# RetNet attention and SwiGLU on one Trainium2 core: the first chunk of the gate's weights loaded later, and products without a use in TensorE's first stops

## The chip, the cores and the metric

The kernel runs on one core of a Trainium2 chip. The metric is the device time of one execution in microseconds (us). Before the change the median of 7 executions is 1141.08 us, from 1139.92 to 1148.08.

A core has a matrix engine (TensorE; in the profile PE, and PEld for its loading of stationary operands), VectorE (DVE), ScalarE (ACT), GpSimd (POOL) and SyncE (SP). Each takes its instructions in an order fixed in the program. In this kernel SP issues nearly all transfers between the chip's memory and the core's own; ScalarE issues a few.

## The reference

Two blocks follow each other. The first is retention without a softmax, with a decay that depends on the head; the second normalizes and applies a gated feed-forward.

```python
# q, k, v: (8, 8, 576, 64) float32: batch, heads, sequence, head size
scores = (1 / sqrt(64)) * q @ k.T
gamma  = 1 - 2 ** (-5 - arange(8))                 # one per head
Dmat   = where(i >= j, gamma ** (i - j), 0)
attn   = (scores * Dmat) @ v
x      = attn.transpose(0, 2, 1, 3).reshape(4608, 512)

xn  = x / sqrt(mean(x * x) + 1e-6) * rms_g
g   = xn @ w_gate                                  # 512 x 1536
out = (g * sigmoid(g) * (xn @ w_val)) @ w_out      # 1536 x 512
```

q, k and v are float32. The three weights arrive in 64-bit floating point (a float32 array times a 64-bit scalar), and the kernel turns them into float32 itself; this is what it calls rounding.

## The kernel before

**Attention jobs.** A job is one batch entry and one pair of heads: 32 jobs of 576 positions. A job runs in chunks of 64 positions with a state carried from chunk to chunk. Its steps, with the line of each: `turn` transposes q and k on TensorE (L228, L234, L242) and ScalarE copies them out of the accumulator banks (L239, L248); `scale_v` multiplies v by the decay on ScalarE (L264); `scores` (L284) and `states` (L304) are products of TensorE; `weigh` masks the scores on VectorE (L316); `sums` carries the states from chunk to chunk on VectorE (L331, L333); `values` (L355) and `carried` (L377) are TensorE's products for the output, and VectorE scales that into x (L397). The scores and states of a job share one set of three accumulator banks, of which there is one, so the next job's `scores` wait for `sums`. `values` of a job is issued in the slot of the next one, and `carried` behind that job's states.

**The feed-forward** works on units of 384 tokens, twelve in all. The first two are multiplied in the plain way (`up_plain`, L614, products of 128x384); the ten others with seven block products in place of eight (`up`, L557, and `across`, L688).

**The start** (function `start`) does the first 8 jobs, which fill units 0 and 1, then the plain products of these two units. In these 8 jobs SP loads everything in an order written out by hand: for each job q, two halves of k, the tails of q and k where they are due, two halves of v, the tail of v (`load_first`, L158, L165, L198). A tail is the last 64 positions; the first tails load is for heads 0 and 1, the second, in job 1, for the six others of the batch entry. Between the jobs come tables and some weights.

**The weights.** They are loaded in 18 chunks of 1024 KB (`load_chunk`, L795): for each third g of the feed-forward's width gate first half, gate second half, value first half, value second half (chunks 0 to 11), then w_out (12 to 17). A 64-bit chunk needs a place of its own while it is rounded, and there are four. `load_chunks(n)` loads on to chunk n as far as places are free.

**Rounding** is a generator, `rounding`, that issues a chunk in steps: the exponent on VectorE (L811), which also enters three operations for ScalarE in a list (Relu, L827); three mantissa steps on VectorE (L838, L843, L848), the third of which needs the three Relus and frees the place, so that a later chunk's load is issued behind it; and the join (L856). `weights(n)` takes n steps, `weights_to(n)` goes on until n chunks are done, `act(n)` issues n of the listed Relus, and all these are called at fixed places of the program. So the place of each step among an engine's other work is fixed.

At the end of job j the kernel calls `turn(j + 1)`, adds the square of x, scales a later v, calls `act(1)`, takes the steps of `weights` for this job, and calls `act(1)` again. In `up_plain` two steps are taken behind each product; the first two products (of the four in a group) use one chunk, the last two the next one. The first group's third product therefore needs chunk 1 joined.

At the very start six products of a matrix of ones with itself run on TensorE into a bank that nobody reads (L920).

Of the kernel before, what the change touches and what calls it, by code (L numbers as in the profile page):

```python
# [14 lines left out]
P = 128  # L15
# [7 lines left out]
def _decay_tables(H, D):  # L23

    pairs = _gamma(H).reshape(H // 2, 2).T
    rows = np.repeat(pairs, D, axis=0)
    pos = np.arange(L)
    p = np.concatenate([pos, pos])  # L30
    gq = rows[:, :, None] ** (pos + L) / np.sqrt(D)
    t = pairs.T[None] ** -p[:, None, None], rows**L, gq, np.roll(gq, D, axis=0)
    return [np.ascontiguousarray(x).astype(np.float32) for x in t]


def _causal_table():

    return np.ascontiguousarray(np.tile(np.triu(np.ones((L, L), np.float32)), (2, 1)))
# [3 lines left out]
def kernel(  # L42
# [11 lines left out]
    nc = tc.nc  # L54
# [33 lines left out]
    def bank(name):  # L88
        return banks.tile([P, 512], F32, tag="b", name=name)
# [9 lines left out]
    ones = const.tile([P, P], F32, name="ones")  # L99
# [117 lines left out]
            out=t, in_=v[b, 2 * hp : 2 * hp + 2, NFULL * P :].rearrange("e p d -> p e d")  # L217
        )

    def turn(j):  # L220

        d = st[j]
        last = bank(f"turn_{j}_t")
        for nm in "qk":
            ps = bank(f"turn_{j}_{nm}")
            for c in range(NFULL):
                if nm == "k":
                    nc.tensor.transpose(  # L228
                        out=ps[:, c * P : c * P + P],
                        in_=d["k"][:, c].rearrange("p e d -> p (e d)"), identity=ident,  # L230
                    )
                    continue
                for e in range(2):
                    nc.tensor.matmul(  # L234
                        ps[side(e), c::NFULL], lhsT=d["q"][:, e, c], rhs=ident,
                        start=True, stop=True,
                    )
            t = d[nm + "T"] = att.tile([P, S], F32, tag=nm + "T", name=f"{nm}T_{j}")
            nc.scalar.copy(out=t[:, : NFULL * P], in_=ps)  # L239
        for i, nm in enumerate("qk"):  # L240
            o = slice(i * TAIL, i * TAIL + TAIL)
            nc.tensor.transpose(  # L242
                out=last[:, o], in_=d[nm + "t"].rearrange("p e d -> p (e d)"),
                identity=ident[:TAIL, :TAIL],
            )
        for i, nm in enumerate("qk"):
            o = slice(i * TAIL, i * TAIL + TAIL)
            nc.scalar.copy(out=d[nm + "T"][:, NFULL * P :], in_=last[:, o])  # L248
# [10 lines left out]
    def scale_v(j):  # L259
        d = st[j]  # L260
        hp = jobs[j][1]
        for e in range(2):
            for t in (d["v"][:, :, e], d["vt"][:, e]):
                nc.scalar.activation(  # L264
                    out=t, in_=t, func=AF.Copy, scale=gv[: t.shape[0], hp, e : e + 1]
                )
# [4 lines left out]
    def side(i):  # L271
        return slice(i * L, i * L + L)
# [489 lines left out]
    for g in range(NG):  # L762
        for m, src in enumerate((moe_w_gate, moe_w_val)):
            for half in range(2):
                n = (half * NH + 2 * g) * P
# [13 lines left out]
    def spare(i):  # L779

        return i % 4 if i < n_up else LATER[i - n_up]

    def load_chunk(i, queue):
        dst, src, rws, cols = chunks[i]
        if src.dtype != F32:
            n = dst.shape[1]
            cols = slice(2 * (cols.start or 0), 2 * cols.stop if cols.stop else None)
            src = src.bitcast(U32)
            at = spare(i)
            dst = free[:, : 4 * DM] if at == 3 else (  # L790
                w_out[:, 4 * at : 4 * at + 4].rearrange("p c f -> p (c f)")
            )
            dst = words_of[i] = dst.bitcast(U32).rearrange("p (c f) -> p c f", c=n)
            waits_at[at] = i
        queue.dma_start(out=dst, in_=src[rws, cols].rearrange("(c p) f -> p c f", p=P))  # L795

    def load_chunks(n, queue=nc.scalar):

        nonlocal n_loads
        while n_loads < min(n, len(chunks)) and waits_at.get(spare(n_loads)) is None:  # L800
            load_chunk(n_loads, queue)
            n_loads += 1
# [90 lines left out]
    def weights(n):  # L893

        for _ in range(n):
            next(steps, None)

    def weights_to(n):

        while n_chunks < min(n, len(chunks)):  # L900
            next(steps)
# [3 lines left out]
    def start():  # L905

        h_of[0] = ffn.tile([P, NF, U], F32, tag="h", name="h_0")
        tables = list(zip((causal, gv, gc, gq, gx), (_causal_table(), *_decay_tables(H, D))))

        def table(i, queue):  # L910
            t, values_ = tables[i]
            src = nc.inline_tensor(values_, name=t.tensor.name + "_table")
            queue.dma_start(out=t, in_=src.ap())

        make_identity(nc, ident)
        nc.scalar.activation(out=tick, in_=mhalf[:1], func=AF.Silu)
        nc.vector.memset(ones, 1.0)
        warm = bank("warm")
        for _ in range(6):
            nc.tensor.matmul(warm[:, :P], lhsT=ones, rhs=ones, start=True, stop=True)  # L920
        first_places.update(find_places())
        load_chunks(1)
        for i in (1, 0, 2):
            table(i, nc.scalar)
        weights(3)
        for j in range(2 * NHP):
            load_first(j, {0: range(2), 1: range(2, H), NHP: range(H)}.get(j))
            if j == 1:
                table(3, nc.sync)
            load_chunks((1, 1, 1, 1, 2, 2, 2, 3)[j], nc.sync)  # L930
        table(4, nc.sync)
        nc.sync.dma_start(out=rms_g, in_=moe_rms_g.rearrange("(c p) -> p c", p=P))
        load_chunks(4, nc.sync)
        turn(0)
        scale_v(0)
        act(3)
        squares = []
        for j in range(2 * NHP):
            slot(j)
            if j + 1 < 2 * NHP:  # L940
                turn(j + 1)
            if squares:
                gather(*squares.pop())
            for i in ((1,), (2,), (3,), (4, 5), (6,), (7,), (), ())[j]:
                scale_v(i)
            if j:
                u, c = divmod(j - 1, NHP)
                squares.append((u, c, square(u, c)))
            act(1)
            if j == 5:  # L950
                norm_1(0)
            elif j == 6:
                norm_2(0)
            weights((2, 0, 0, 1, 1, 1, 1, 0)[j])
            if j == 4:
                gather(*squares.pop())
            elif j == 5:
                diagonals(0)
            act(1)
        gather(*squares.pop())  # L960
        load_qk(2 * NHP)
        load_kv(2 * NHP)
        made = combine_out()
        for m, g in [(m, g) for g in range(NG) for m in range(2)]:
            for u in range(2):
                weights_to(4 * g + 2 * m + 1)
                for i, _ in enumerate(up_plain(u, m, g)):
                    if not (u or m or g):
                        if i == 0:
                            values(2 * NHP - 1)  # L970
                            carried(2 * NHP - 1)
                            gather(1, NHP - 1, square(1, NHP - 1))
                        elif i == 1:
                            norm_1(1)
                        elif i == 2:
                            diagonals(1)
                        elif i == 3:
                            norm_2(1)
                    weights(2)
                    act(1)  # L980
                    if u and m and g == NG - 1:
                        weights_to(len(chunks))
                        next(made, None)
                    if i == 1:
                        weights_to(4 * g + 2 * m + 2)
        for _ in made:
            pass
        for blk, t in first_blocks.items():
            keep(blk, t)
        rest = across(1)  # L990
        next(rest)
        following(2 * NHP - 1)
        for i, _ in enumerate(rest):
            if i == 1:
                norm_0(2)
                differences(0)
            elif i == 2:
                norm_1(2)
                diagonals(2)
            elif i == 4:  # L1000
                norm_2(2)
        rest = across(0)
        next(rest)
        combine(1)
        slot(8, rest=False)
        following(8)
        for _ in rest:
            pass
        combine(0)
        slot(9)  # L1010
        following(9)
# [18 lines left out]
    with tc.manual_schedule():  # L1030
# [4 lines left out]
        for u in range(2, NU):  # L1035
# [11 lines left out]
            for i, _ in enumerate(rest):  # L1047
                if i == 0 and turns:
                    prepare_next(turns.pop())
                if i == 2:  # L1050
                    behind(u, 6)
                    at, n = SLOTS[u % 3]
# [33 lines left out]
```

## Time and profile before

| what | value |
|---|---|
| median of 7 executions | 1141.08 us |
| lowest, highest | 1139.92, 1148.08 us |
| the profiled execution | 1141.87 us |
| its span, first to last instruction | 1140.1 us |
| mean granted clock of TensorE | 0.997 |
| ScalarE's stop before its first copy of q (L239) | 6.70 us |
| VectorE's stop before the exponent of chunk 0 (L811) | 5.69 us |
| ScalarE's stop for the v of job 5 | 1.57 and 0.45 us |
| first product of the feed-forward (L614) starts at | 59.41 us |

The page gives the busy time of each engine, the span in 40 slices, and the costliest groups. The chain of waits follows the work that ended last back to its start, each piece with its start, its length and what it was; "issue" is time for which the profile shows no cause. In the timeline each row has start, length, engine, line, operation, tiles (out<-in), shape and count, and in brackets the idle time ahead of it with what ended it. Times are in us from the first instruction.

### The profile page before, as it was taken

What the parts mean: (1) busy time and instruction counts of PE and PEld (TensorE: products, weight loads), DVE (VectorE), ACT (ScalarE), POOL (GpSimd) and SP (SyncE); (2) the same over time, 40 slices, a digit from 0 to 9 for tenths busy, and PEclk for the clock granted to TensorE, in tenths of its full rate; (3) what the DMA queues carried; (4) which work ended last, traced back from release to release, by engine and by line L of the source; (5) the groups of instructions that cost most, each with busy time, mean ns of one, the idle gap of its engine ahead of it and who ended that gap; (6) DMA issues with size and microseconds to landing.
All of it is one profiled execution on the core that took longest, in us unless ns stands there. A gap on an engine that the chain in (4) does not pass through costs nothing.

```text
span 1140.1 us, 24713 instructions
## 1 busy us (share of the span) xinstructions
PE 1119.1 (98%) x10470; PEld 1046.2 (92%) x10470; DVE 726.6 (64%) x1431; ACT 258.9 (23%) x508; POOL 39.7 (3%) x64
## 2 busy tenths in 40 slices
PE   7899999999999999999999999999999999999998
PEld 6755557999999999999999999999999999999998
DVE  5788868655685685375767676466676666446352
ACT  5546642002212211211221121121121220120210
POOL 0000000470000000000000000000000000000000
PEclk9999999999999999999999999999999999999999
DMA  9764336335464475053444555216436503303304
GB/s 204 209 183 152 110 113 205 62 66 131 102 134 88 125 151 152 1 117 92 103 126 62 127 135 122 113 32 119 115 81 142 139 26 97 126 1 100 124 1 111
DMA packets 292942, 125.40 MB, mean 110 GB/s; under 512 B 270432, under 2 KB 275808, under 8 KB 292832
## 3 DMA queue, kind: packets, MB, share of 16 engines
q1 hardware_dynamic: 282688, 107.66, 38.4%
q10 hardware_dynamic: 10144, 16.16, 4.5%
q8 instruction: 82, 1.34, 0.5%
q14 instruction: 28, 0.23, 0.1%
HBM read 108.83 MB, written 14.94 MB: 109 GB/s over the span
## 4 chain that ended last, share of the span: by engine, by line
PE 93%; DMA 2%; DVE 2%; ACT 1%; issue 1%; SPq 0%; DVEq 0%; POOL 0%; POOLq 0%; ACTq 0%
PE x L557 14%; PE w L557 14%; PE z L557 14%; PE xo L688 8%; PE wo L688 8%; PE zo L688 8%; PE up L614 8%; PE y L557 7%; PE yo L688 4%; PE av L355 2%; PE av L377 2%; PE s L284 1%; PE s L304 1%; DMA w_gate<-in_moe_w_out_dram 1%; PE ms L475 1%
## 5 line engine op out<-in xcount | busy, mean ns | idle before, releaser
L581 ACT COPY m<-x 128x384 f32<-128x384 f32 x60 | 28.8, 479 | 338.8 <-PE x L557 338.8
L688 PE MATMUL xo<-h,w_out 128*128 128x192 f32 x528 | 90.3, 328 | 0.0
L557 PE MATMUL w<-sums,w_val 128*128 128x192 f32 x480 | 88.6, 328 | 0.3
L557 PE MATMUL x<-x,w_val 128*128 128x192 f32 x480 | 88.7, 328 | 0.0
L557 PE MATMUL z<-x,w_gate 128*128 128x192 f32 x480 | 87.9, 326 | 0.7 <-DVE u L564 0.7
L557 PE MATMUL x<-x,w_gate 128*128 128x192 f32 x480 | 88.5, 328 | 0.0
L557 PE MATMUL z<-x,w_val 128*128 128x192 f32 x480 | 87.8, 326 | 0.0
L557 PE MATMUL w<-sums,w_gate 128*128 128x192 f32 x480 | 87.8, 326 | 0.0
L688 PEld LDWEIGHTS xo<-h,w_out 128*128 128x128 f32 x528 | 85.9, 190 | 0.6
L688 PE MATMUL wo<-h,w_out 128*128 128x192 f32 x504 | 85.3, 326 | 0.0
L564 DVE TENSOR_TENSOR u<-m,y 128x384 f32<-128x384 f32 x60 | 33.2, 553 | 79.1 <-PE y L557 79.1
L688 PEld LDWEIGHTS wo<-h,w_out 128*128 128x128 f32 x504 | 82.5, 190 | 0.0
L557 PEld LDWEIGHTS w<-sums,w_val 128*128 128x128 f32 x480 | 79.2, 190 | 2.7 <-DVE c L564 2.7
L557 PEld LDWEIGHTS z<-x,w_gate 128*128 128x128 f32 x480 | 79.6, 190 | 1.0 <-issue 1.0
L557 PEld LDWEIGHTS x<-x,w_val 128*128 128x128 f32 x480 | 79.1, 190 | 0.6
L557 PEld LDWEIGHTS x<-x,w_gate 128*128 128x128 f32 x480 | 79.3, 190 | 0.5
L557 PEld LDWEIGHTS z<-x,w_val 128*128 128x128 f32 x480 | 79.6, 190 | 0.0
L557 PEld LDWEIGHTS w<-sums,w_gate 128*128 128x128 f32 x480 | 79.5, 190 | 0.0
L564 DVE TENSOR_TENSOR h<-u,w 128x384 f32<-128x384 f32 x60 | 33.1, 551 | 69.5 <-PE w L557 69.4
L576 ACT ACTIVATE h<-h 128x384 f32<-128x384 f32 x90 | 47.0, 523 | 89.5 <-DVE h L564 89.5
L614 PE MATMUL up<-x,w_gate 128*128 128x384 f32 x192 | 63.3, 488 | 0.9 <-DVE x L526 0.7
L614 PE MATMUL up<-x,w_val 128*128 128x384 f32 x192 | 62.7, 487 | 0.1
(187 smaller groups left out, 1769.8 us busy)
## 6 DMA issues: line engine op xcount, KB each, us to landing
w_out<-w_blocks SPq DMA_DIRECT2D x70, 768.0 KB, 5.0
out_dram<-o SPq DMA_DIRECT2D x368, 24.0 KB, 1.6
qraw<-in_q_dram SPq DMA_DIRECT2D x96, 72.0 KB, 2.8
kraw<-in_k_dram SPq DMA_DIRECT2D x96, 72.0 KB, 2.8
k<-in_k_dram SPq DMA_DIRECT2D x48, 128.0 KB, 3.0
v<-in_v_dram SPq DMA_DIRECT2D x48, 128.0 KB, 3.1
w_out<-in_moe_w_gate_dram ACTq DMA_DIRECT2D x5, 1024.0 KB, 5.7
w_out<-in_moe_w_out_dram ACTq DMA_DIRECT2D x3, 1024.0 KB, 5.0
```

The costliest lines, as they stand in the source:

```text
L284: nc.tensor.matmul(s[side(odd), e, i * L : i * L + L], lhsT=d["kT"][side(e), c * L : c * L + L], rhs=d["qT"][side(e), c * L : c * L + L], ...
L304: nc.tensor.matmul(o[side(e)], lhsT=d["k"][side(odd), i, e], rhs=d["v"][side(odd), i, e], start=True, stop=True,)
L355: mm = nc.tensor.matmul(av[odd][column(j, odd, e), i * L : i * L + L], lhsT=d["v"][side(odd), i, e] if c < NC - 1 else d["vt"][:, e], rhs= ...
L377: mm = nc.tensor.matmul(av[odd][column(j, odd, e), i * L : i * L + L], lhsT=d["sum"][side(e), c - 1], rhs=d["qT"][side(e), c * L : c * L + L],
L475: nc.tensor.matmul(s, lhsT=ones, rhs=y, start=True, stop=True)
L557: nc.tensor.matmul(ps[:, i * HU : i * HU + HU], lhsT=w_up[m][:, 2 * blk + c, cut], rhs=t_of[u][blk][:, c], start=(start and i == c == 0), ...
L564: nc.vector.tensor_tensor(out=o, in0=a, in1=pairs_of(ps), op=ALU.add)
L576: nc.scalar.activation(out=o, in_=c, func=AF.Silu)
L581: nc.scalar.copy(out=s1, in_=pairs_of(x_))
L614: nc.tensor.matmul(ps[:, :U], lhsT=w_up[m][:, 4 * half + c, i * P : i * P + P], rhs=x_of[u][:, c], start=(c == 0), stop=(c == NHP - 1),)
L688: nc.tensor.matmul(ps[:, i * HU : i * HU + HU], lhsT=a[:, c, i * P : i * P + P], rhs=rhs[:, c], start=(start and i == c == 0), stop=False, ...
```

## The change

Four things are edited.

1. Chunk 0, formerly loaded on ScalarE's queue at the start, is loaded on SP's queue behind the loads of job 1 and the table gq.
2. The three steps of rounding that were taken before the first job are taken in the jobs: the numbers of steps by job are 1, 2, 1, 1, 1, 1, 1, 0 in place of 2, 0, 0, 1, 1, 1, 1, 0. `act(3)` before the first job stays, and finds its list empty there. So the 8 jobs end with 8 steps taken, where it was 9.
3. `turn` takes a pair of numbers, `waits`: so many products of ones with ones are issued between the transposes of q and those of k, and so many behind the transposes of the tails. They go to the bank of the first six.
4. `turn(0)` is called with (4, 4), the others with none.

```diff
+    warm_of = {}
+
+    def warm_up(n):
+
+        if not warm_of:
+            warm_of[0] = bank("warm")
+        for _ in range(n):
+            nc.tensor.matmul(
+                warm_of[0][:, :P], lhsT=ones, rhs=ones, start=True, stop=True
+            )
+
-    def turn(j):
+    def turn(j, waits=(0, 0)):
 
         d = st[j]
         last = bank(f"turn_{j}_t")
         for nm in "qk":
+            if nm == "k":
+                warm_up(waits[0])
             ps = bank(f"turn_{j}_{nm}")
...
                 identity=ident[:TAIL, :TAIL],
             )
+        warm_up(waits[1])
         for i, nm in enumerate("qk"):
...
         nc.vector.memset(ones, 1.0)
-        warm = bank("warm")
-        for _ in range(6):
-            nc.tensor.matmul(warm[:, :P], lhsT=ones, rhs=ones, start=True, stop=True)
+        warm_up(6)
         first_places.update(find_places())
-        load_chunks(1)
         for i in (1, 0, 2):
             table(i, nc.scalar)
-        weights(3)
         for j in range(2 * NHP):
             load_first(j, {0: range(2), 1: range(2, H), NHP: range(H)}.get(j))
             if j == 1:
                 table(3, nc.sync)
-            load_chunks((1, 1, 1, 1, 2, 2, 2, 3)[j], nc.sync)
+            load_chunks((0, 1, 1, 1, 2, 2, 2, 3)[j], nc.sync)
         table(4, nc.sync)
         nc.sync.dma_start(out=rms_g, in_=moe_rms_g.rearrange("(c p) -> p c", p=P))
         load_chunks(4, nc.sync)
-        turn(0)
+        turn(0, (4, 4))
         scale_v(0)
         act(3)
...
-            weights((2, 0, 0, 1, 1, 1, 1, 0)[j])
+            weights((1, 2, 1, 1, 1, 1, 1, 0)[j])
```

## The prediction

> **What bounds the kernel now.** I read the page first: TensorE (PE) is busy 98% of the span, and only the first three of its 40 slices fall short. So time can be won or lost only where PE waits, and that is the start. Slices are 28.5 us.
>
> ```profile
> span 1140.1 us, 24713 instructions
> PE 1119.1 (98%) x10470; PEld 1046.2 (92%) x10470; DVE 726.6 (64%) x1431; ACT 258.9 (23%) x508; POOL 39.7 (3%) x64
> PE   7899999999999999999999999999999999999998
> ```
>
> Then the chain of waits for the first 24 us. It runs through two landings, the second of them the last rows of job 1's v, at 17.69; not before this do scaling and job 1's states go on. Only from 19.2 is the chain PE's.
>
> ```profile
> 3.74 5.38 DMA first_sums<-in_v_dram
> ...
> 12.16 5.53 DMA w_val<-in_v_dram
> 17.70 0.02 issue
> 17.72 0.35 ACT w_val L264
> 18.07 0.41 ACT first_sums L264
> 18.48 0.04 issue
> 18.52 0.62 PE s L304 x25
> ```
>
> Then the timeline of VectorE (DVE). The start of L316 (weigh) is the clock of the jobs: 12.44, 19.23, 24.45, 29.69, 35.64, 45.16, 51.87, 59.18. Ahead of it DVE idles about 1.05 us in jobs 1 to 3, which is all the room that moved rounding finds there.
>
> ```profile
> 19.23 0.89 DVE L316 SCALAR_TENSOR_TENSOR ret<-s,causal 128x320 f32<-128x320 f32 x2 [1.09 <-PE last L304]
> 24.45 0.89 DVE L316 SCALAR_TENSOR_TENSOR ret<-s,causal 128x320 f32<-128x320 f32 x2 [1.05 <-PE s L304]
> 29.69 0.89 DVE L316 SCALAR_TENSOR_TENSOR ret<-s,causal 128x320 f32<-128x320 f32 x2 [1.08 <-PE s L304]
> ```
>
> Then the chain again for 35 to 46 and for 64 to 112: PE stops 2.06 us for nothing that the profile shows, then runs at half speed (the stretch 37.87 to 41.29 has a granted clock of 0.50); and the second pair of gate products begins at 68.16, just as chunk 1's last step (L856, 66.80, 1.22 us) ends at 68.02.
>
> ```profile
> 35.82 2.06 issue
> 37.87 1.75 PE av L377 x26
> 39.63 1.87 PE turn_q L234 x16
> ...
> 66.92 1.16 ACT w_gate L827
> 68.08 0.09 issue
> 68.16 5.40 PE up L614 x16
> ```
>
> From 74.91 on PE is gapless but for 0.67 us at 175.86, so what the start saves by then reaches the end.
>
> **What the Trainium skill says.** "DMA: Bandwidth & Descriptors", section "Issuing engines are not separate DMA queues": transfers of all issuers share the same 16 engines. The trace agrees: beside ScalarE's 1 MB, issued at 0.93, the first k (128 KB) took 6.2 us to land, against 2.7 for such a k later. "TensorE: Matmul & The Clock Gate", Part 1: the array runs at half clock until a window of about 3.4 us is busy, and falls back after an idle one; the window runs freely. Here the first full grant is at 13.98, and the half-clock spell lasts 3.42 us. The same page's queue note has VectorE strictly first in, first out. The trace has no counterexample; the cost of exponent(0) below rests on it. "Runtime: NRT & Kernel Launch", "Instruction fetch mechanics": blocks of 256 instructions are fetched by DMA. Stops without a shown cause at 35.82, 49.5 and 58.05 fit this; no row proves it.
>
> **The change part by part.** All sums are against the profiled execution: 1141.87, which is the span 1140.1 and 1.8 around it; the median 1141.08 is 0.8 lower.
>
> *Loads.* Chunk 0 (1 MB) leaves ScalarE's queue, goes behind job 1's loads and the gq table on SP's, ahead of job 2's. Nothing is transferred less. What can be gained is idling: before, SP stood 2.4 us (4.89 to 7.30) for the first k's landing. After, SP issues sixteen loads at about 0.6 us each from 0.73, to 10.5; with the 2.4 us that the small v tail takes to land, job 1 is in at 12.8, not 17.7. gq takes 0.5, chunk 0 about 2.9 (chunk 1 came 2.5 after its predecessor, chunk 3 4.0): it is in at 16.2. Before, the same bytes were in at 17.9 (gq, 12.81 + 5.1). So all later loads come 1.7 us sooner; bounds 0 and 2.4 (the whole stop of SP). ScalarE's three tables no longer wait for others' landings, and its first copy not until 8.92.
>
> *Products without use.* Eight, 16 passes; the six at the start took 2.93 us cold, so four cost 1.95 cold, about 1.0 warm. Four fill the wait for k, four the copies. If the clock rises near 7, scores(0) begins at 9.2 instead of 10.05; if it stays cold, at 11.2. Either is covered by the next point: 5.7 us later sums(0) end, at 17 at the latest. Cost between -0.5 and +0.5; I take 0.
>
> *Rounding chunk 0.* Before, L811, L838, L843 ran before job 0, and L848, L856 (2.45) behind it. Now exponent (0.69) stands at the end of job 0 on DVE's queue and waits for chunk 0; weigh(1), sums(1), the x of job 0 stand behind it, and values(1) and scores(2) on PE wait for these. So weigh(1) is at 16.2 + 0.7 = 16.95 (before 19.23). Then, with durations of the rows: weigh and sums 3.3, x 0.9, mantissa 1.9: weigh(2) 23.05 (-1.4). 3.25, 0.9, third step 1.2: weigh(3) 28.4 (-1.3). 3.3, 0.9, gather 0.5, join 1.2: weigh(4) 34.3 (-1.3). So DVE, not PE, sets these jobs: 2.3 us won at job 1, 1.0 given back.
>
> *Job 5.* Before, ScalarE was held by job 5's v (landed 37.80), square and one relu, then by turn_q (41.5). Now v lands at 36.1; scaling 0.75 and square 0.45 give 37.3, with no relu, as chunk 1's exponent comes a job later. turn_q(5): sums(3) end at 31.7, scores, states, carried 2.0, the same stop 2.06, turn_q 1.05: 36.8. Copies start at 37.3 (before 41.58), and 3.66 later, as before, weigh(5): 41.0, so -4.1. Without the stop and slow spell before would have had its copies at 40.05: part of this, 1.5, is luck of that execution. I take -4.0. The rest of the jobs keeps it: two relus more in job 5 lie in ScalarE's idle 3.7 us before 53.56.
>
> *One step later.* The jobs take 8 of the rounding's steps instead of 9, so chunk 1's third step (L848, 1.22), with two loads on ScalarE's queue, falls behind the first gate product; join(1) comes behind norm_1 and ends at about 69.45 instead of 68.02. The second pair of products needs it: +1.4, on the path. Bounds 0.7 and 2.0, after DVE's idle 0.25 and how the small steps fall.
>
> *Late.* At 173.55 ScalarE's relu of chunk 17 blocked a Silu and PE stopped 0.67. Now exponent(17) comes one product later, its relu behind that Silu: -0.7, bounds -0.7 and +2.6 (one product's time, if the load chain falls behind instead).
>
> *Fetches.* Eight products are 32 instructions; block ends shift 16 matmul passes forward. The stop of 0.81 at 58.05 is on PE's path; half of it, -0.4, bounds -0.8 and +2.
>
> Sum: -4.0 + 1.4 - 0.7 - 0.4 = -3.7; 1141.87 - 3.7 = 1138.2. As part of the slow spell must be in other executions of before too, I leave it so and say **1138.0**.
>
> **Rivals.**
> 1. *The loads come no sooner.* If transfer time alone bounds them, chunk 0 is in at 17.9, weigh(1) at 18.6, and DVE's extra steps make weigh(2) 24.65 (+0.2), weigh(4) 35.95 (+0.3); job 5 gains only the relu and the slow spell, weigh(5) 43.0 (-2.15). With +1.4 and -0.7: 1140.4. For it: DMA's share is about 1 from 10 on. Against: 0.85 and less around 8 to 10, when SP had stood.
> 2. *The late step rules, slower.* Chunk 15 to 17 hang on each other (DMA 4.91, 5.19, 4.92 with four steps between, 146 to 174). If the lag of one step puts each load behind one product more, PE loses 2.6 at about 176 on top of 1.4 at 68. With only 0.6 won at weigh(1): 1141.9 - 0.6 + 4.0 = 1145.3. It decides once the lag costs more than the start saves. Against it: the steps between the three loads are the same in number.
> 3. *The products don't warm.* Scores(0) at 11.2, sums(0) at 17.0, weigh(1) about 18.4, 1.4 later than mine; of that the load-bound job 5 hides half: 1138.8.
>
> **How the numbers follow.** Forecast 0.57 (own range 1135.5 to 1140.0), rival 1 0.20, rival 2 0.13, rival 3 0.10. The bound of 0.3% is 3.4 us, about what a measurement of this kernel can tell from no change; so faster means below 1137.7, slower above 1144.5. The forecast lies near that line: 0.40 of its 0.57 I put below it (the bounds on that side are loads 2.4 sooner and fetch stops gone), 0.16 in between and 0.01 on the slow side; of rival 3 half lies on each side of that line. Faster 0.40 + 0.05 = 0.45; same 0.16 + 0.20 + 0.05 = 0.41; slower 0.13 + 0.01 = 0.14. Range: 1134.5 (all lower bounds near enough) to 1141.5 (rival 1 with the upper bound of the join).
>
> **What would show it.** L811 for chunk 0 waiting for its load until about 16.2 and L316 starting right behind it; L316 of jobs 2 to 4 without idle time; copies of job 5 at 37 to 38; first gate product at about 55; a stop of PE near 64 to 65 before the third, ended by L856; none near 172. Wrong, if chunk 0 lands after 18.5, if L316 of job 5 comes later than 43, or if PE stops over 2 us anywhere between 60 and 190.

## The result, and the profile after

After the change the median is 1148.99 us (12 executions, 1146.54 to 1153.19), against 1142.44 for the kernel before in the same comparison (31 executions). The ratio is 1.0057, with a 95% interval from 1.0041 to 1.0072: the change costs about 6.5 us. The prediction was 1138.0, with a range to 1141.5.

The profiled execution of after took 1150.76 us, 8.9 more than that of before. In it the first product of the feed-forward starts at 66.96 (before 59.41), and from there to the end of the span it is 1082.0 us (before 1080.7). So 7.55 us are lost before that product, and 1.3 behind it.

The page of after: the span, TensorE's busy time and passes, and its busy share and granted clock in 40 slices of 28.7 us.

```profile
span 1149.0 us, 24740 instructions
PE 1126.5 (98%) x10486; PEld 1052.9 (92%) x10486; DVE 726.3 (63%) x1431; ACT 259.2 (23%) x508; POOL 39.6 (3%) x64
PE   8789999999999999999999999999999999999998
PEclk7899999999999999999999999999999999999999
```

The passes are 16 more, which are the eight products. Yet TensorE is busy 7.4 us longer (1126.5 against 1119.1), and their own work is only 2.3 us of it (two groups of 1.16 us): the same matmuls ran at half clock for longer. Beside the cold start and the last microseconds, which both kernels have, the spells of half clock in the records are 15.70 to 29.35, 36.18 to 46.42 and 77.14 to 80.55, together 27.3 us. In before it was one, of 3.4. (The cold start, which the clock row counts as full, lasts to 5.46 in after and to 13.98 in before.)

The chain of waits of after, up to job 2. Columns: start, length, what it was; "SPq" is SP's own time for issuing a transfer.

```profile
9.77 0.51 SPq L165
...
10.32 0.61 SPq L198
...
10.97 1.67 SPq L928
...
12.68 0.43 SPq L810
...
13.16 6.99 DMA h<-in_q_dram
...
20.19 1.98 PE turn_q L248 x16
22.17 1.06 PE turn_k L242 x4
```

In before the chain ran here through landings of v. Now it runs from 5.44 to 13.12 through SP's issuing, one transfer behind the other: the last halves and tail of v of job 1 (L165, L198), the table gq (L928, whose issue alone takes 1.67), chunk 0 (L810), and then q of job 2, which lands at 20.15. In before that q was in at 18.66. `turn_q` of job 2 then runs at half clock, 1.98 instead of 1.09.

VectorE's timeline of after: the exponent of chunk 0 (L826) and the starts of `weigh` (L331) of jobs 1 to 3.

```profile
18.18 0.69 DVE L826 TENSOR_SCALAR w_gate<-w_out 128x1024 uint32<-128x1024 uint32 x1 [4.89 <-DMA w_out<-in_moe_w_gate_dram]
18.79 0.88 DVE L331 SCALAR_TENSOR_TENSOR ret<-s,causal 128x320 f32<-128x320 f32 x2
...
27.27 0.89 DVE L331 SCALAR_TENSOR_TENSOR ret<-s,causal 128x320 f32<-128x320 f32 x2 [2.46 <-PE s L319]
...
33.45 0.89 DVE L331 SCALAR_TENSOR_TENSOR ret<-s,causal 128x320 f32<-128x320 f32 x2 [0.89 <-PE s L319]
```

The exponent waits for its chunk until 18.18, and `weigh` of job 1 stands right behind it: 0.4 sooner than in before. By job 2 it is 2.8 later, by job 3 3.8. The wait of 2.46 in job 2 is for TensorE's products, whose q came late and which ran at half clock; it isn't the rounding that holds `weigh` there.

The chain again, where TensorE is about to turn q of job 4, and where the third gate product starts.

```profile
33.41 0.81 PE av L392 x26
34.22 3.12 issue
37.34 0.59 PE av L392 x5
37.92 1.90 PE turn_q L248 x16
...
75.42 1.23 DVE w_gate L871
76.64 0.14 issue
76.78 7.09 PE up L629 x16
```

The stop without a cause at 34.22 is 3.12 long. It isn't the stop of 2.06 that the prediction speaks of: that one stood in the next job, ahead of q of job 5. At this place, some 15 passes further on in TensorE's order, before stood 0.38 us (from 31.26). The half clock that begins in it lasts three times as long as that of before (10.2 us against 3.4), and `weigh` of job 4 comes at 45.26 instead of 35.64. At 76.78 the products wait for the join of chunk 1 (L871), the wait that the prediction priced at 1.4; TensorE's timeline puts its idle time at 1.48.

### The profile page after: what moved, and what is told of

Its sections match the earlier page's. It is cut to its first block, busy times and chain, and to the rows that moved or that the text cites. A ratio compares the mean times of both kernels' runs of the same rounds, so it can differ in the third digit from the quotient of the medians.

```text
span 1149.0 us, 24740 instructions
## 1 busy us (share of the span) xinstructions
PE 1126.5 (98%) x10486; PEld 1052.9 (92%) x10486; DVE 726.3 (63%) x1431; ACT 259.2 (23%) x508; POOL 39.6 (3%) x64
## 4 chain that ended last, share of the span: by engine, by line
PE 91%; DVE 4%; DMA 2%; ACT 1%; issue 1%; SPq 1%; DVEq 0%; POOLq 0%; POOL 0%; ACTq 0%
PE w L572 14%; PE x L572 14%; PE z L572 13%; PE zo L703 8%; PE wo L703 8%; PE xo L703 8%; PE up L629 7%; PE y L572 7%; PE yo L703 4%; PE av L370 2%; PE av L392 2%; PE s L299 2%; PE s L319 1%; DMA w_gate<-in_moe_w_out_dram 1%; PE turn_q L248 1%
## 5 line engine op out<-in xcount | busy, mean ns | idle before, releaser
L596 ACT COPY m<-x 128x384 f32<-128x384 f32 x60 | 28.8, 479 | 337.1 <-PE x L572 337.1
L629 PEld LDWEIGHTS up<-x,w_gate 128*128 128x128 f32 x192 | 37.0, 194 | 28.3 <-issue 1.7
```

The costliest lines, as they stand in the source:

```text
L596: nc.scalar.copy(out=s1, in_=pairs_of(x_))
L629: nc.tensor.matmul(ps[:, :U], lhsT=w_up[m][:, 4 * half + c, i * P : i * P + P], rhs=x_of[u][:, c], start=(c == 0), stop=(c == NHP - 1),)
```

## The experiments

A theory for each part of the change, and what would speak against it:

- *Loads.* Chunk 0 behind job 1 makes the later loads late, because SP alone cannot issue fast enough to keep the DMA engines busy. In some expectations this is theory A. Rival: bytes are bytes, and the place doesn't matter.
- *Rounding.* The exponent and mantissa steps in the jobs hold `weigh` (theory C).
- *The step that is missing* costs TensorE's stop at the third gate product.
- *Products* (theory B). The eight products cost by their own time or by what they do to the clock (theories G and H), or because their instructions shift the places where instructions are fetched (theory F).

Each ratio below is to the kernel before, executed on the same chip in turn, with its 95% interval; 0.001 is 1.14 us.

**After without the products.**

```diff
-        turn(0, (4, 4))
+        turn(0)
```

> The changed kernel without its eight useless products (before 1142.4, changed 1149.0). Theory A (loads: chunk 0 on SyncE's queue leaves the transfer engines half idle from 4 to 8 us, job 2's q lands at 20.1 instead of 18.7, TensorE stands and its clock halves): the products change little, 1149 +- 1.5, and job 2's q still lands at about 20. Theory B (products: they shift the instruction blocks or the clock's window and cause the slow spells): back to 1143 or 1144.

Measured 1.0040 [1.0029, 1.0051]: both theories missed the number. The products cost 0.0017, or 1.9 us, and most of the loss is elsewhere. Theory A missed in one thing more. The q of job 2 isn't late here: it lands at 18.66, as in before, and TensorE turns it sooner than before did, though at half clock. First this kernel, then before:

```profile
18.71 1.97 PE L248 MATMUL turn_q<-ident,h 128*64 128x128 f32 x16 [2.13 <-DMA h<-in_q_dram]
```

```profile
20.07 1.09 PE L234 MATMUL turn_q<-ident,h 128*64 128x128 f32 x16
```

So the late q in the chain of after does not follow from the place of chunk 0's load alone.

**After with chunk 0 loaded at the start on ScalarE's queue again.** Rounding stays in its new places.

```diff
+        load_chunks(1)
         for i in (1, 0, 2):
...
-            load_chunks((0, 1, 1, 1, 2, 2, 2, 3)[j], nc.sync)
+            load_chunks((1, 1, 1, 1, 2, 2, 2, 3)[j], nc.sync)
```

> The changed kernel with chunk 0's load put back on ScalarE's queue at the start; rounding in the jobs and the products stay. Theory A: job 2's q lands near 18.7 again, no stop before turn_q of job 2, and of the 6.5 us lost at least 4 come back: 1142.5 to 1145. Theory C (the rounding's new places: exponent of chunk 0 at the end of job 0, and everything one step later): nothing of that is touched, 1148 to 1149. Theory B: 1148 to 1149.

Measured 1.0031 [1.0019, 1.0044], 1144.61 us, as theory A said. The load's place costs 0.0026, 3.0 us: the largest part.

**After with a ninth step, in job 7.**

```diff
-            weights((1, 2, 1, 1, 1, 1, 1, 0)[j])
+            weights((1, 2, 1, 1, 1, 1, 1, 1)[j])
```

> The changed kernel with a ninth step of rounding in job 7, so that join of chunk 1 comes behind the first product again. All theories: the stop of 1.5 us before the third gate product goes, and with it the slow clock behind it where that fell (77 to 80.5 in the changed profile, 1.7 us). Theory A: 1.5 to 3 us come back, 1146 to 1147.5. Theory C: most of the 6.5 come back, 1143 to 1145.

Measured 1.0042 [1.0028, 1.0057]; the stop before the third gate product is 0.70 instead of 1.48. The difference of 0.0015 is 1.7 us. The intervals of the two ratios overlap, so this difference alone doesn't show the price; a second pair follows below.

**Before with the products alone.**

```diff
-        turn(0)
+        turn(0, (4, 4))
```

> The kernel before with the eight products alone. Theory A: the clock rises some 5 us earlier, but job 1 still waits for its v at 17.7, so 1142.4 +- 1. Theory B: the products make the slow spells, 1146 to 1149.

Measured 1.0017 [1.0007, 1.0028]: the same price as in after, without any of the rest. It isn't a steady 1.9 us. Of the 22 executions 11 took at most 1142.28 us and 11 at least 1143.87, with none between; of before, in the same comparison, 6 of 67 took over 1143. The profiled execution took 1144.18, so it is one of the longer ones.

**Before with the same eight products of one column.** As many instructions, so the shift is the same.

```diff
-    def warm_up(n):
+    def warm_up(n, n_cols=P):
...
-                warm_of[0][:, :P], lhsT=ones, rhs=ones, start=True, stop=True
+                warm_of[0][:, :n_cols], lhsT=ones, rhs=ones[:, :n_cols], start=True, stop=True
...
-                warm_up(waits[0])
+                warm_up(waits[0], 1)
...
-        warm_up(waits[1])
+        warm_up(waits[1], 1)
```

> The kernel before with the eight products of the change at their places, but one column each: as many instructions, hardly any time on TensorE and no warming. The eight full products alone gave a ratio of 1.0017 to before, about 1.9 us. Theory F (fetch: the 32 instructions shift the blocks in which TensorE's instructions are fetched, so that a late block falls into carried of job 3 and TensorE stops 3.1 to 3.6 us there instead of 2.06): 1.001 to 1.002, and the stop in that place is over 3 us. Theory G (it is the products' own time or the clock they move): 1.000 +- 0.0007, stop as before.

Measured 0.9997 [0.9986, 1.0009]: nothing. TensorE's timelines of the two, full products first, then those of one column (L227; L298 is the first `scores`):

```profile
5.76 1.16 PE L227 MATMUL warm<-ones 128*128 128x128 f32 x8
...
8.89 1.16 PE L227 MATMUL warm<-ones 128*128 128x128 f32 x8
9.98 0.81 PE L298 MATMUL s<-qT,kT 64*64 64x64 f32 x40
```

```profile
5.98 1.87 PE L227 MATMUL warm<-ones 128*128 128x1 f32 x8
...
9.54 1.86 PE L227 MATMUL warm<-ones 128*128 128x1 f32 x8
11.33 1.34 PE L298 MATMUL s<-qT,kT 64*64 64x64 f32 x40
```

This says more than was asked. Those of one column take longer (1.87 for four, against 1.16), with TensorE cold until 17.46, and the first scores come 1.35 later. That costs nothing: `weigh` of job 1 starts at 19.18, where it was 19.23 in before. So neither the time of the products nor the shift is what costs by itself. Two things differ in the profiles. One is the clock: with full products it is full from 5.48 on, falls back from 15.72 to 19.13, and again from 32.79 to 43.03. The other is a stop of TensorE at the same place and time of both (30.4 us), which is much longer with the full products:

```profile
34.02 0.58 PE L391 MATMUL av<-qT,sum 64*64 64x64 f32 x6 [3.59 <-issue]
```

```profile
31.77 0.39 PE L391 MATMUL av<-qT,sum 64*64 64x64 f32 x6 [1.40 <-issue]
```

What these stops are is told behind the last experiment.

**After without the products and with the ninth step,** so that the load's place and the rounding's places are left.

```diff
-        turn(0, (4, 4))
+        turn(0)
...
-            weights((1, 2, 1, 1, 1, 1, 1, 0)[j])
+            weights((1, 2, 1, 1, 1, 1, 1, 1)[j])
```

> The changed kernel without the products and with a ninth step in job 7: what is left is chunk 0's load on SyncE's queue behind job 1, and its rounding in the jobs. If the three prices add (load 3.0 us from 1.0057 less 1.0031, products 1.9, late step 1.7 out of 6.5): about 1.0026, and job 2's q lands at 18.7 to 20.2. Theory C (rounding's places) gives the same here; the next but one run tells it from the load.

Measured 1.0027 [1.0014, 1.0040]. The parts add up, as far as intervals of 0.0013 either way can tell. Against after without the products (1.0040), from which it differs by the ninth step alone, it gives the missing step a price of 0.0013: the second pair. Here too the price of the load's place isn't a steady one: 13 of the 22 executions took over 1143 us, of before 11 of 59, and they reach from 1139.81 to 1150.20. The profiled one (1142.47) is among the shorter. In it q of job 2 lands at 18.82.

**The same, with v and its tails of jobs 0 and 1 issued by ScalarE,** so that two engines issue at the start.

```diff
-    def load_first(j, tails):
+    def load_first(j, tails, v_queue=nc.sync):
...
+            queue = v_queue if nm == "v" else nc.sync
...
-                nc.sync.dma_start(
+                queue.dma_start(
...
-            load_first(j, {0: range(2), 1: range(2, H), NHP: range(H)}.get(j))
+            load_first(
+                j, {0: range(2), 1: range(2, H), NHP: range(H)}.get(j),
+                nc.scalar if j < 2 else nc.sync,
+            )
```

> As the load alone, but v of jobs 0 and 1 with its tails is issued by ScalarE, which has nothing to do then. Theory A in its sharp form (SyncE's issuing, some 0.6 us for each load, starves the transfer engines from 4 to 8 us): the engines move over 250 GB/s there instead of 135, chunk 0 lands at 16 to 17 instead of 18, job 2's q by 18.5, and the ratio falls from 1.0026 to 1.000 or less, perhaps below before. Theory A2 (bytes come no sooner whoever issues, since landings bound the eight transfers in flight): the ratio stays above 1.002.

Measured 0.9994 [0.9985, 1.0004]: the whole loss of the load is gone, 0.0033 or 3.8 us, by who issues the v of two jobs, and 1 of 22 executions took over 1143 us. Chunk 0 was awaited until 16.7, as expected. The view by windows shows what a second issuer does at the start. Columns: window, its length, busy us (and count) of PE, PEld, DVE, ACT and POOL, the clock, the DMA engines' busy share, GB/s. First before, then after, then two issuers:

```profile
4.00:8.00 4.00, 2.05 (x17) 1.58 (x16) 1.15 (x2) 0.00 (x0) 0.00 (x0) 1.00 1.19 305
```

```profile
4.00:8.00 4.00, 4.00 (x35) 3.52 (x35) 0.00 (x0) 1.20 (x4) 0.00 (x0) 1.00 0.63 135
```

```profile
4.00:8.00 4.00, 3.22 (x23) 2.49 (x22) 0.00 (x0) 0.00 (x0) 0.00 (x0) 1.00 0.90 204
```

Between 4 and 8 us before moved 305 GB/s, after 135 (the load alone 144): less than half, with the engines busy at 0.63. Two issuers moved 204, not the 250 expected. The missing 170 GB/s over 4 us are 0.68 MB. But after makes up most of it: with its next three such windows (216, 205 and 316 GB/s against 190, 193 and 202 in before) it is 0.17 MB behind at 20 us, by the windows from 0 on. So one issuer left the engines idle at the start, and that it matters who issues is shown; how 0.17 MB become 3 us the windows don't show. SP's timeline has the order of the loads, here of before and then of two issuers: the q of job 2 (L158) is issued at 13.46 in before, at 13.16 in after (only 0.3 sooner, and now with chunk 0 right ahead of it), and at 11.02 with two issuers.

```profile
12.81 0.61 SPq L913 DMA_DIRECT2D gq<-gq_table  x1
13.46 0.43 SPq L158 DMA_DIRECT2D h<-in_q_dram  x1
```

```profile
9.89 0.61 SPq L929 DMA_DIRECT2D gq<-gq_table  x1
10.55 0.43 SPq L811 DMA_DIRECT2D w_out<-in_moe_w_gate_dram  x1
11.02 0.51 SPq L158 DMA_DIRECT2D h<-in_q_dram  x1
```

The v of job 5, four jobs on, lands at 37.8 in before, 38.9 in after, 38.8 in the kernel with the load's place alone, 37.7 with two issuers. ScalarE waits for it 1.57 and 0.45 us in before, 2.95 and 0.27 with the load alone, and not at all in after, where job 5 comes later for other reasons. (On theory A2: in before, where SP stood from 4.89 to 7.30, eight transfers were issued and not landed, six of SP and two of ScalarE.)

**The rounding's new places alone** (as the last but one, with chunk 0 loaded early by ScalarE).

```diff
+        load_chunks(1)
         for i in (1, 0, 2):
...
-            load_chunks((0, 1, 1, 1, 2, 2, 2, 3)[j], nc.sync)
+            load_chunks((1, 1, 1, 1, 2, 2, 2, 3)[j], nc.sync)
...
-        turn(0, (4, 4))
+        turn(0)
...
-            weights((1, 2, 1, 1, 1, 1, 1, 0)[j])
+            weights((1, 2, 1, 1, 1, 1, 1, 1)[j])
```

> Chunk 0 loaded early by ScalarE as before, no products, nine steps: only the places of rounding chunk 0 differ from before (in the jobs instead of ahead of them). Theory A: 1.000 +- 0.001, since VectorE finds 1.05 us of room in each of jobs 1 to 3 and no longer waits for a load. Theory C: 1.002 to 1.004.

Measured 0.9995 [0.9983, 1.0006]. The new places cost nothing; against the kernel with the late load (1.0027) the load's place is worth 0.0032 here.

**Two attempts to gain from this,** with the ninth step in job 4 instead of job 7, where it would remove the rest of the stop before the third gate product: once with two issuers, once with the early load.

```diff
-            weights((1, 2, 1, 1, 1, 1, 1, 1)[j])
+            weights((1, 2, 1, 1, 2, 1, 1, 0)[j])
```

> Two issuers and chunk 0 behind job 1, as in the run of that name (0.9994), with the ninth step taken in job 4, where VectorE stood about 3 us for a square, in place of job 7. If the step's place is what leaves the stop of 0.76 us before the third gate product, the stop falls to 0.2 and the ratio to 0.9988 or less: faster than both. If VectorE's order in jobs 4 and 5 is the tighter one, the ratio stays or rises to 1.000.

> Chunk 0 early by ScalarE, no products, rounding in the jobs with the ninth step in job 4. With step in job 7 this gave 0.9995, with a stop of 0.78 us before the third gate product. If that stop is on the path: 0.9989; with the loads of before it tells what the rounding's places alone can bring.

Measured 1.0006 [0.9993, 1.0020] and 1.0003 [0.9991, 1.0014]: neither gained. The chain of the first of them shows the step in its place, with ScalarE's Relu and no join ahead of the third product,

```profile
65.44 1.16 ACT w_gate L843
66.60 0.09 issue
66.69 5.40 PE up L630 x16
```

and the stop there is 0.16 in both, but no time came of it. So a stop at this place isn't always paid for in full. Of the kernels tried none is faster than before by more than its interval.

**The two issuers with the step in job 4, and the products.**

```diff
-        turn(0)
+        turn(0, (4, 4))
```

> The run before this one with the eight full products. Theory H (a TensorE that is warm early only waits longer for the loads, its clock falls, and a slow spell of 3 us comes in about half the executions instead of one in six): 1.5 to 2 us more than without them, whatever the loads. Theory I (the products cost because of this load order alone): no difference beyond 0.001, since the stops they bridge are shorter here.

Measured 1.0025 [1.0015, 1.0035], 0.0019 more than without the products: the third pair with the same price, with the loads arranged in a third way. That is the size theory H gave; 18 of 22 executions took over 1143 us, without the products 4 of 14.

**Before with two issuers:** chunk 0 first on ScalarE's queue, as before has it, and v of jobs 0 and 1 behind it. The edit of `load_first` is the one above.

> The kernel before, chunk 0 first on ScalarE's queue, with v of jobs 0 and 1 issued by ScalarE behind it. If two issuers help by themselves: 0.999 or less. Theory A: the engines are already full from 4 to 8 us here (385 and 224 GB/s), so nothing is won; ScalarE's copies come no sooner: 0.9995 to 1.001.

Measured 1.0053 [1.0032, 1.0074], a miss by 5 us. The v of job 0 now stands behind 1 MB on ScalarE's queue, the first `weigh` comes at 17.2 instead of 12.4, and TensorE is at half clock for 23.9 us. So here the second issuer did harm, with what it issues put behind a long transfer.

**The products taken apart, in before.** One product of 512 columns in each stop in place of four of 128 (the work of all eight, a quarter of the shift):

```diff
-    def warm_up(n):
+    def warm_up(count, n=1):
...
-                warm_of[0][:, :P], lhsT=ones, rhs=ones, start=True, stop=True
+                warm_of[0][:, : n * P].rearrange("p (n c) -> p n c", c=P), lhsT=ones,
+                rhs=ones.unsqueeze(1).to_broadcast([P, n, P]), start=True, stop=True
...
-                warm_up(waits[0])
+                warm_up(waits[0], 4)
...
-        warm_up(waits[1])
+        warm_up(waits[1], 4)
...
-        turn(0, (4, 4))
+        turn(0, (1, 1))
```

> Before with one product of 512 columns in each of the two stops in place of four of 128: the same work for TensorE as in e4_products_alone, and 4 more passes instead of 16. If the work itself costs (TensorE warm at 5.5 and later slow again, or its own time), the ratio is 1.0015 to 1.002 as there. If the 16 passes cost through the place of the block fetches, 0.9995 to 1.0005, and the stops without a shown cause between 20 and 67 us are back at about 3.6 us in sum.

Measured 1.0013 [1.0000, 1.0027], nearer to the eight full products than to none, though the interval reaches down to 1. The stops without a cause sum to 5.5 us, not 3.6. Then the four in the wait for k alone, `turn(0, (4, 0))`, and the four in the wait for the copies alone, `turn(0, (0, 4))`:

> Before with the four products in the wait for k only. If warming early is what costs, this is the part that warms: the clock is full near 5.5 and the ratio is about 1.0015. If time on the path to the first scores costs, this part costs nothing (the landing of k ends the wait), 1.000.

> Before with the four products in the wait for the copies only. If warming early is what costs, 1.0000 to 1.0005, the clock being full no sooner than about 9. If time on the path to the first scores costs, all of it is here: scores of job 0 at 11 or later, ratio 1.0015.

Measured 1.0001 [0.9988, 1.0013] and 1.0000 [0.9989, 1.0012]: neither shows a price. The last two expectations both fall as far as they give one half the whole 1.9 us; that each half carries half of it (0.0009) lies within all the intervals. The clock is full at 6.36 and at 6.21, so the four in the wait for the copies do not leave it cold until 9, as was expected. The scores of job 0 start at 9.86 and 9.77, much as with both (9.98), so their start isn't what costs either. What differs again is the clock. The windows from 14 to 18 us (columns as above), of the eight products and of the four in the wait for k:

```profile
14.00:18.00 4.00, 2.88 (x81) 2.48 (x81) 3.39 (x6) 3.24 (x9) 0.09 (x1) 0.72 1.10 225
```

```profile
14.00:18.00 4.00, 2.46 (x93) 1.95 (x94) 3.70 (x7) 3.25 (x9) 0.09 (x1) 1.00 0.90 202
```

With four, the clock is full near 6.3, falls back from 9.8 to 13.2, in job 0, and is full from there on. With eight it holds over job 0, and falls back in job 1, from 15.7. Over all the profiles, one of each kernel:

| kernels | ratio | half clock before 31 us | fourth packet, us after chunk 1's first |
|---|---|---|---|
| before, chunk 0 early with the rounding moved, the same with the step in job 4, products of one column | 0.9995 to 1.0003 | cold until 14 to 17.5, then full | -1.1 to 0.3 |
| two issuers, the same with the step in job 4, four products (twice) | 0.9994 to 1.0006 | a spell that ends by 13.5, then full | -0.2 to 0.2 |
| after, after without products, with the ninth step, the load alone, eight products, two wide ones, two issuers with products | 1.0013 to 1.0057 | a spell that begins between 15.7 and 21.1 | 2.9 to 5.3; the load alone -1.4 |

Two kernels that are slow don't fit the last row: after with the load put back (1.0031, its spells at 38.4 and 52.1), and before with two issuers (1.0053, half clock from 8.0 to 18.2). And a spell of 3.4 us at half clock can cost at most half of that, and in job 1 less, as the jobs wait for loads. Nor is an early full clock the products' doing alone: after without the products is full at 4.92, the load alone at 5.47. And the mean granted clock, on record for every execution, is 0.9959 with the eight products and 0.9954 in before, 0.9956 for two issuers with them and 0.9949 without: no more half clock in sum. Only with the late load of chunk 0 is it lower with them (0.9906 in after, without them 0.9935). So the third column says where the slow kernels differ, not how the 1.9 us come about.

**What the stops without a cause are.** The packets in the traces tell. The page of before has a queue of its own for instructions:

```profile
q8 instruction: 82, 1.34, 0.5%
```

These are 82 packets of 16 KB. TensorE has 20940 products and loads of stationary operands, 255 for each packet. In all 17 traces together TensorE has 65 stops without a cause of 0.2 us or more that end between 18 and 80 us, and each of them ends 1.2 to 1.7 us after the end of such a packet. So TensorE waits there for its instructions. How long it waits depends on when the packet comes. Below is the row of q8 for 28.8 to 30.2 us with the products of one column, then for 31.4 to 32.5 with the full ones, where there was none from 28.2 on:

```profile
q8 instruction: 1, 0.02, 6.0%
```

```profile
q8 instruction: 1, 0.02, 5.5%
```

This is the fourth packet, from 28.83 and from 31.47, and the stops that it ends are the two shown above, 1.40 and 3.59. At that time chunk 1 (1 MB) is on its way: its packets begin at 28.54 and 28.20. The last column of the table has this distance for every kernel. Where the fourth packet starts ahead of chunk 1 or at most 0.3 us behind its beginning, the stop it ends is 0.4 to 1.4 us long; where it starts 2.9 us or more behind, 2.1 to 3.9 us. (Of the two kernels outside the rows, before with two issuers has 4.6, and after with the load put back -1.2, but a later packet starts 1.3 us behind the beginning of chunk 3 and ends a stop of 2.65.) That reads as if instructions and chunk 1 met at the DMA engines, and a few tenths of a microsecond decided which goes first. It would fit executions that fall into two groups. But it rests on one profile of each kernel, and no run moved chunk 1. And stops as long stand at the fifth packet too, with no chunk on its way and at no price (3.34 with the four in the wait for k). So it is a candidate for how the products and the load's place cost time, and isn't shown.

## Why the prediction was wrong

*Loads, the step that failed.* The prediction let chunk 0 land at 16.2 and all later loads come 1.7 sooner, with bounds of 0 and 2.4. It was 18.16, against the 17.9 at which before had the same bytes, and by job 5 the loads were 1.1 later. Its first half held: SP did issue the loads of jobs 0 and 1 back to back, to 10.93 (10.5 said), and job 1 was in 2.9 sooner (14.84, though 12.8 was said). The error is in "Nothing is transferred less. What can be gained is idling". The 1 MB on ScalarE's queue was what kept the DMA engines busy while SP, at about 0.6 us for 128 KB, could not. With it gone they were busy at 0.63 from 4 to 8 us, and the 1 MB came on top later, behind a gq whose issue took 1.67 where 0.5 had been put for the whole of it. The lower bound of 0 for the gain was no bound. What this cost by itself was 3.0 us (in after) to 3.7 (alone), and a second issuer took it away: this is shown. The way from there to the 3 us isn't: the bytes are nearly made up by 20 us, and without the products q of job 2 was on time. What is left are the v of job 5, 1.0 later, and more half clock: the mean granted clock of the load alone is 0.9939 over its executions, of before 0.9956.

The Trainium skill, "DMA: Bandwidth & Descriptors", section "Issuing engines are not separate DMA queues", says that a second issuer saves only sequencer time, usually small. The prediction leaned on its first half, that all share the same engines. Here the second half was wrong in size: the sequencer's time was the bound in these 4 us.

*Products, the second step that failed.* Put at 0, between -0.5 and +0.5, with 5.7 us of waiting as cover. The cover was there: products of one column delay the first scores to 11.33 for nothing. And TensorE was warm early, as said (full at 5.46). Yet they cost 1.9 us, in three pairs of kernels. Rival 3, that they don't warm, looked at the wrong side. "TensorE: Matmul & The Clock Gate", Part 1, has the clock fall back after an idle window of about 3.4 us; the lengths of the spells agree, 3.42, 10.24 and 13.65 being one, three and four of these. That the window has to be idle does not: ahead of the fall at 37.87 in the kernel before, TensorE was busy 1.36 us of the 3.41 from 34.46 on, with a stop of 2.06 only. That warming early made room for falling back later, in the waits for loads, fits the profiles; the mean clocks of all executions show more of it only with the late load. The late fourth packet is another candidate and wasn't tested. So the path to the 1.9 us stays open.

*Rounding chunk 0.* The order was right: L826 waits for the load, and L331 starts behind it. Set to the chunk's real landing the rule gives 18.16 + 0.7 = 18.9, and 18.79 was measured. That VectorE would set jobs 2 to 4 was not so in after, where TensorE came later still. The new places by themselves cost nothing (0.9995).

*Job 5.* The gain of 4.0 rested on the loads, and on the stop staying at 2.06 with one spell behind it. The loads came later, a stop of 3.12 stood one job earlier with a spell of 10.2, and `weigh` of job 5, which was put at 41.0 and not to be later than 43, came at 52.9. ScalarE no longer waited for v there, so the 1.0 by which it was late cost nothing in this execution. The prediction put 1.5 of its gain down to chance in the profiled execution of before. It wasn't that: with the early load and the rounding moved that stretch looks much the same (a stop of 2.6, one spell).

*One step later.* +1.4 said, 1.48 measured as a stop (0.16 in before), 1.7 and 1.5 as a price in two pairs. Right, and at its place, as far as those intervals tell.

*Late.* -0.7 said. The 64 products with the value's weights that hold the place, in TensorE's timelines of before and after:

```profile
167.90 21.13 PE L614 MATMUL up<-x,w_val 128*128 128x384 f32 x64
```

```profile
178.21 20.80 PE L629 MATMUL up<-x,w_val 128*128 128x384 f32 x64
```

The same 64 take 0.33 less, so what before lost there is gone, at half the size put. The loss of 2.6 in rival 2 did not come: the direction of that rival was right, its place was not.

*Fetches.* -0.4 said, and that no row proves them; the packets of q8 do. The stops without a cause of 0.5 us and more between 20 and 67 us sum to 3.6 in before and 5.2 in after, but 5.6 with the products of one column, which cost nothing. So their sum shows no price of the shift.

*Two readings.* The page's row has the first two slices short and the last, not the first three. And from 74.91 on TensorE stands not only at 175.86 but also 0.70 us ahead of 255.99, 0.88 ahead of 270.94 and 0.76 ahead of 292.69. No term of the sum rests on either.

Rival 1, loads that come no sooner, was right on the step that mattered, and still 8.6 us too low: it kept 2.15 of job 5's gain, and the products at nothing.

In sum: 3.0 for the load, 1.9 for the products, 1.7 for the step, 0 for the rounding are 6.6, against 6.5 measured. Each of these differences is known to about 2 us either way, so that they meet so closely is in part luck.

## What to carry to other kernels

A large transfer from a second issuer at the start is not in the way merely because it shares the DMA engines: look at the GB/s of the windows while the main issuer works through small transfers, and don't take the large one away unless something else fills that time. Where a sum of changes is predicted, give each part a lower bound that comes from a resource's rate, not from the assumption that moving bytes is neutral. Products without a use are to be measured, not taken as free because they stand in a wait: eight of them cost 1.9 us here. And where the times of one kernel fall into two groups, one profile shows one of them; look at the list of times before a profile is read as the cause.

## What was not expected of the hardware

- In the first 10 us SP took 0.4 to 0.7 us to issue a transfer of 32 to 256 KB. Later it was often more: 1.67 for the 128 KB gq in after (0.61 in before), 1.25 and 1.52 for a q in before, 3.00 for one with two issuers (at 15.47). Why wasn't tried.
- Eight passes of one column took 1.87 us cold, as long as eight of 128 columns that ran mostly cold (1.85, two issuers with the products); warm those took 1.16. With one column TensorE stayed cold until 17.46, with 128 it was full at 5.48, and in kernels without either at 4.92 (after without products) to 13.98 (before).
- TensorE waited for its instructions up to 3.9 us between 30 and 53 us, a different time in every kernel. After stops of over 3 us the half clock lasted 10.2 us in after and in before with eight products, but wasn't there at all in before with four in the wait for k (a stop of 3.34 at 38.5).
- Eight full products cost 1.9 us; four in either place showed no price, within 1.5 us.
